# A linear-attention and MoE kernel on one core: bonus term moved to VectorE, state kept block-diagonal, and a scheduler that models the port, the DMA queue and the matmul banks

## The chip, the cores and the metric

The kernel runs on one core of a Trainium2 chip. The metric is the device time of one execution in microseconds. The kernel before takes 244.26 us (median of four runs, 243.75 to 245.22). "PE" is TensorE's matmul stream, "PEld" its weight loads, "DVE" is VectorE, "ACT" ScalarE, "POOL" GpSimd and "SP" SyncE, which issues most of the DMAs. SBUF is the on-chip memory that the engines work from, PSUM the one that PE writes its products to; a "bank" is one of PSUM's parts. A "span" is the length of the profiled execution; times inside it start at 0.

## The reference, cut to what matters

The first half is a recurrent attention with a decay `w` per head and channel and a bonus `u` for the current token; the second half is a two-layer MoE block with a leaky ReLU.

```python
# batch 4, heads 8, sequence 768, head_dim 48
for t in range(S):
    cur = einsum('bhd,bhe->bhde', u * k[t], v[t])
    y[t] = einsum('bhd,bhde->bhe', r[t], state + cur)
    state = w * state + einsum('bhd,bhe->bhde', k[t], v[t])
x = y as 3072 tokens x 384
out = leaky(x @ w_in) @ w_out          # w_in 384 x 2048, w_out 2048 x 384
```

Both kernels cut the sequence into 24 stages of 128 tokens (six for each batch element). A stage scales r and k by powers of w (`q_h`, `k_h`), forms masked products between tokens on PE (`ATm`), adds what comes through the state (`s_bd`) and the bonus (`vs`), and transposes the result into `xT`, from which the MoE matmuls read.

## The kernel before

The program is a list of operations with their dependences, a priority, and a duration guessed by the author. A list scheduler runs over it once, on the host, and fixes the order of instructions on every engine. On the chip each engine works through its list in that order. The guessed durations matter only in that they decide the order.

```python
op("DVE", q_h = raw_r * qdec, 490, base + 2)            # 490 ns is what the scheduler is told
op("DVE", k_h = raw_k * kdec, 490, base + 3)
op("POOL", v_sb <- DMA of v, cast to bf16, 1000, base - 150)
op("POOL", rk  = raw_r * raw_k, 540, base + 4)          # f32, 128 x 384
op("POOL", rku = rk * u_tab,    540, base + 5)
op("DVE", s_b = sum over channels of rku, 490, base + 6)
op("POOL", vs = v_sb * s_b, 540, base + 7)
...                                                     # cut: transposes, ATm
op("DVE", z_st = p_kx + s_st, 290, base + 12)           # state, 48 wide per head
op("DVE", s_st = z_st * wlt, 190, base + 12)
for p in range(2):                                      # into the block-diagonal tile
    op("DVE", tensor_copy(s_bd[64*p:64*p+64, :, D*p:D*p+D], s_st[64*p:64*p+64]), 150, base + 13)
...                                                     # cut: y_sb, xT
bk = ring[0] % NMOE; ring[0] += 1                       # three MoE banks in turn
TILES = [(0, 256), (256, 256)] + [(512 * i, 512) for i in range(1, 6)]
```

## Time and profile before

| | before |
|---|---|
| median time | 244.26 us |
| VectorE busy, last `y_sb` starts | 133.2 us, 159.2 us |
| last `xT` copy starts, from there to the end (MoE alone) | 160.3 us, 82.6 us |
| mean granted PE clock | 0.965 |

From the page of the kernel before: busy time by engine, then five rows of the 40 slices of the span (each digit is a busy share in tenths; `PEclk` is the granted clock in tenths).

```profile
PE 182.6 (75%) x1595; PEld 108.8 (45%) x1608; DVE 133.2 (55%) x230; ACT 111.1 (46%) x194; POOL 100.0 (41%) x115
...
PE   0111543776838886978687779999999999999995
...
DVE  1702887889999999999998999820000000000000
...
POOL 8800296695896786985756834100000000000000
PEclk9999999997985999979997999999999999999999
DMA  6999499986491886977586800012001001101121
```

VectorE stands at 8 or 9 from slice 8 to slice 26 and then stops; PE is full only afterwards. So the kernel has two phases in series: attention at VectorE's pace, then MoE at PE's pace. The same by stretches (kernel before; busy microseconds of each engine in each stretch):

```profile
24.00:90.00 66.00, 42.85 (x492) 30.59 (x493) 59.91 (x95) 25.94 (x53) 48.94 (x52) 0.92 0.84 105
90.00:160.20 70.20, 57.16 (x633) 32.82 (x642) 66.71 (x121) 37.34 (x62) 40.79 (x43) 0.95 0.55 71
160.20:242.90 82.70, 79.62 (x442) 43.19 (x442) 0.00 (x0) 38.46 (x68) 0.00 (x0) 1.00 0.13 48
```

The first column after the stretch is its length; then PE, PE's weight loads, DVE, ACT and POOL. From 24 to 160.2 us VectorE works 126.6 of 136.2 us, PE 100.0. PE was idle for the other 36 us. Up to about 48 us no whole MoE tile was finished; in some 25 of the 36 us, counted from the trace, MoE matmuls of finished tiles were waiting for their turn in PE's fixed list. At 128 us, 17 stages were copied into `xT`; their whole tiles hold 82 us of MoE work (an estimate at the 2.4 columns a ns measured below), and 28 us of it had been done.

VectorE's time is not all work. By tile, kernel before (minimum/median/maximum duration in ns, first and last start in us):

```profile
L387 DVE COPY s_bd<-s_st x40: 189/264/3198, 24.6 to 156.6; 64x192 bf16<-64x192 bf16 x40
L330 DVE TENSOR_TENSOR q_h<-raw_r,qdec x24: 541/559/2684, 7.3 to 151.5; 128x384 bf16<-128x384 f32 x24
L332 DVE TENSOR_TENSOR k_h<-raw_k,kdec x24: 541/617/3082, 9.3 to 154.3; 128x384 bf16<-128x384 f32 x24
L406 DVE TENSOR_TENSOR y_sb<-p_y,vs x24: 542/548/558, 31.1 to 159.2; 128x384 bf16<-128x384 f32 x24
```

The means are 744 ns (`s_bd`), 888 (`q_h`) and 970 (`k_h`). `y_sb`, which reads one operand from PSUM, never takes more than 558. What stretches them is visible in order of time (kernel before; start, duration, engine):

```profile
91.62 0.55 DVE L406 TENSOR_TENSOR y_sb<-p_y,vs 128x384 bf16<-128x384 f32 x1
92.09 2.10 DVE L387 COPY s_bd<-s_st 64x192 bf16<-64x192 bf16 x2
92.09 0.84 POOL L340 TENSOR_TENSOR vs<-v_sb,s_b 128x384 f32<-128x384 bf16 x1
92.88 0.99 POOL L336 TENSOR_TENSOR rku<-rk,u_tab 128x384 f32<-128x384 f32 x1
94.01 1.03 POOL L334 TENSOR_TENSOR rk<-raw_r,raw_k 128x384 f32<-128x384 f32 x1
94.22 1.23 DVE L330 TENSOR_TENSOR q_h<-raw_r,qdec 128x384 bf16<-128x384 f32 x1
```

The two copies take about 0.4 us together when they run alone. Here they take 2.10 us and end 0.3 us after GpSimd's `vs` and `rku`; the next product waits for GpSimd's `rk` in the same way.

### The profile page before, as it was taken

What the parts mean: (1) busy time and instruction counts of PE and PEld (TensorE: products, weight loads), DVE (VectorE), ACT (ScalarE), POOL (GpSimd) and SP (SyncE); (2) the same over time, 40 slices, a digit from 0 to 9 for tenths busy, and PEclk for the clock granted to TensorE, in tenths of its full rate; (3) what the DMA queues carried; (4) which work ended last, traced back from release to release, by engine and by line L of the source; (5) the groups of instructions that cost most, each with busy time, mean ns of one, the idle gap of its engine ahead of it and who ended that gap; (6) DMA issues with size and microseconds to landing.
All of it is one profiled execution on the core that took longest, in us unless ns stands there. A gap on an engine that the chain in (4) does not pass through costs nothing.

```text
span 242.9 us, 3961 instructions
## 1 busy us (share of the span) xinstructions
PE 182.6 (75%) x1595; PEld 108.8 (45%) x1608; DVE 133.2 (55%) x230; ACT 111.1 (46%) x194; POOL 100.0 (41%) x115
## 2 busy tenths in 40 slices
PE   0111543776838886978687779999999999999995
PEld 0111422554626643544344445565455446545562
DVE  1702887889999999999998999820000000000000
ACT  4711120573624534846431658624941971593211
POOL 8800296695896786985756834100000000000000
PEclk9999999997985999979997999999999999999999
DMA  6999499986491886977586800012001001101121
GB/s 131 196 195 205 82 136 173 131 96 70 89 126 34 83 130 99 129 87 85 77 94 136 98 3 0 3 57 72 3 30 68 32 3 65 66 0 35 65 97 66
DMA packets 82034, 20.31 MB, mean 84 GB/s; under 512 B 75872, under 2 KB 81248, under 8 KB 82016
## 3 DMA queue, kind: packets, MB, share of 16 engines
q1 hardware_dynamic: 53520, 14.36, 27.4%
q0 software_dynamic: 27936, 5.51, 26.5%
q10 hardware_dynamic: 560, 0.20, 0.3%
q8 instruction: 12, 0.20, 0.3%
q14 instruction: 6, 0.05, 0.1%
HBM read 20.84 MB, written 4.72 MB: 105 GB/s over the span
## 4 chain that ended last, share of the span: by engine, by line
PE 43%; DVE 36%; DMA 7%; POOL 5%; issue 5%; SPq 3%; ACT 1%; POOLq 0%
PE p_moe L450 22%; PE p_moe L431 15%; DVE s_bd L387 10%; DVE k_h L332 7%; DMA raw_k<-in_k_dram 7%; DVE ATm_0 L363 4%; DVE ATm_1 L363 4%; DVE y_sb L406 3%; DVE s_b L338 2%; DVE q_h L330 2%; SPq L326 2%; POOL rk L334 2%; PE p_t L347 2%; POOL rku L336 2%; DVE s_st L384 1%
## 5 line engine op out<-in xcount | busy, mean ns | idle before, releaser
L431 PE MATMUL p_moe<-xT,w_in_sb 128*128 128x512 bf16 (+1 forms) x323 | 74.1, 369 | 0.5 <-issue 0.2
L450 PE MATMUL p_moe<-w_out_sb,gT 128*128 128x384 bf16 x384 | 68.3, 329 | 0.1
L436 ACT ACTIVATE gT<-p_moe 128x512 bf16<-128x512 f32 (+1 forms) x112 | 58.7, 538 | 19.6 <-PE p_moe L431 15.9
L450 PEld LDWEIGHTS p_moe<-w_out_sb,gT 128*128 128x128 bf16 x384 | 36.8, 99 | 23.1 <-issue 0.5
L431 PEld LDWEIGHTS p_moe<-xT,w_in_sb 128*128 128x128 bf16 x336 | 32.7, 104 | 25.4 <-issue 1.1
L352 ACT ACTIVATE qkT<-p_t 128x1024 bf16<-128x1024 bf16 x24 | 24.5, 1023 | 42.4 <-PE p_t L347 42.4
L340 POOL TENSOR_TENSOR vs<-v_sb,s_b 128x384 f32<-128x384 bf16 x24 | 21.5, 894 | 45.8 <-DVE s_b L338 45.5
L347 PE MATMUL p_t<-ident,q_h 128*128 128x128 bf16 x96 | 10.9, 246 | 29.0 <-DVE k_h L332 28.7
L454 ACT ACTIVATE o_sb<-p_moe 128x384 f32<-128x384 f32 x24 | 11.8, 490 | 43.2 <-PE p_moe L450 43.1
L387 DVE COPY s_bd<-s_st 64x192 bf16<-64x192 bf16 x40 | 29.8, 744 | 0.7
L332 DVE TENSOR_TENSOR k_h<-raw_k,kdec 128x384 bf16<-128x384 f32 x24 | 23.3, 970 | 7.3 <-DMA raw_k<-in_k_dram 7.2
L330 DVE TENSOR_TENSOR q_h<-raw_r,qdec 128x384 bf16<-128x384 f32 x24 | 21.3, 888 | 9.5 <-DMA raw_r<-in_r_dram 6.4
L328 POOL DMA_DIRECT2D v_sb<-in_v_dram x24 | 22.5, 939 | 8.7 <-PE p_y L400 4.1
L334 POOL TENSOR_TENSOR rk<-raw_r,raw_k 128x384 f32<-128x384 f32 x24 | 25.4, 1058 | 1.2 <-DMA raw_k<-in_k_dram 0.5
L336 POOL TENSOR_TENSOR rku<-rk,u_tab 128x384 f32<-128x384 f32 x24 | 24.9, 1036 | 0.1
L414 ACT ACTIVATE xT<-p_kx 128x384 bf16<-128x384 bf16 x24 | 11.8, 490 | 20.5 <-PE p_kx L410 20.3
L347 PEld LDWEIGHTS p_t<-ident,q_h 128*128 128x128 bf16 x96 | 6.3, 107 | 32.7 <-DVE k_h L332 32.0
L363 DVE TENSOR_TENSOR ATm_0<-p_a,mask_f 128x512 bf16<-128x512 f32 x24 | 16.4, 683 | 1.7 <-PE p_a L358 1.4
L410 PE MATMUL p_kx<-ident,y_sb 128*128 128x128 bf16 x72 | 8.9, 239 | 10.8 <-DVE y_sb L406 10.6
L363 DVE TENSOR_TENSOR ATm_1<-p_a,mask_f 128x512 bf16<-128x512 f32 x24 | 16.3, 679 | 0.1
L406 DVE TENSOR_TENSOR y_sb<-p_y,vs 128x384 bf16<-128x384 f32 x24 | 13.2, 548 | 1.7 <-PE p_y L400 1.6
L394 PE MATMUL p_y<-s_bd,qkT 128*128 128x96 bf16 x80 | 7.6, 223 | 8.5 <-DVE s_bd L387 8.3
(42 smaller groups left out, 134.2 us busy)
## 6 DMA issues: line engine op xcount, KB each, us to landing
raw_r<-in_r_dram SPq DMA_DIRECT2D x24, 192.0 KB, 2.8
raw_k<-in_k_dram SPq DMA_DIRECT2D x24, 192.0 KB, 3.4
out_dram<-o_sb SPq DMA_DIRECT2D x24, 192.0 KB, 1.9
v_sb<-in_v_dram POOLq DMA_DIRECT2D x24, 96.0 KB, 4.0
w_in_sb<-in_moe_w_in_dram POOLq DMA_DIRECT2D x6, 256.0 KB, 7.9
w_out_sb<-in_moe_w_out_dram POOLq DMA_DIRECT2D x4, 384.0 KB, 8.7
u_tab<-in_u_dram ACTq DMA_DIRECT2D x1, 192.0 KB, 4.2
lnw<-in_w_dram SPq DMA_DIRECT2D x1, 192.0 KB, 4.0
```

What stands on the lines that cost most here:

```text
L328: op("POOL", lambda: [G.dma_start(vv[:, :, :], src(v))], 1000, base - 150, w=[f"v{vi}"], dma=(f"v{vi}", 16), lat=2600)
L330: op("DVE", lambda: V.tensor_tensor(qh[:, :, 0:D], rr[:, :, :], qdec[:, :, :], ALU.mult), 490, base + 2, w=[f"q{pi}"], r=[f"rr{ri}", "qdec"])
L332: op("DVE", lambda: V.tensor_tensor(kh[:, :, 0:D], rk_[:, :, :], kdec[:, :, :], ALU.mult), 490, base + 3, w=[f"k{pi}"], r=[f"rk{ri}", "kdec"])
L334: op("POOL", lambda: G.tensor_tensor(rk[di][:, :, :], rr[:, :, :], rk_[:, :, :], ALU.mult), 540, base + 4, w=[f"t1{di}"], r=[f"rr{ri}", f" ...
L336: op("POOL", lambda: G.tensor_tensor(rku[di][:, :, :], rk[di][:, :, :], u_tab[:, :, :], ALU.mult), 540, base + 5, w=[f"t2{di}"], r=[f"t1{d ...
L347: last = PE.transpose(p_t[:, 512 * x + 128 * i:512 * x + 128 * i + 128], t[:, 2 * i:2 * i + 2, :].rearrange("p h e -> p (h e)"), ident[:, :])
L352: op("ACT", lambda: ACT.activation(T[:, :, :, :].rearrange("p a i t -> p (a i t)"), p_t[:, :], AF.Copy), 900, base + 9, w=[f"T{di}"], r=[" ...
L363: op("DVE", lambda p=p: V.tensor_tensor(ATm[di][p][:, :, :], p_a[p][:, :].rearrange("p (i t) -> p i t", t=L), mask_f[:, :].unsqueeze(1).to ...
L387: op("DVE", lambda p=p: V.tensor_copy(s_bd[1 - zc][64 * p:64 * p + 64, :, D * p:D * p + D], s_st[1 - zc][64 * p:64 * p + 64, :, :]), 150, ...
L431: op("PE", lambda m=m, fb=fb, bk=bk: PE.matmul(p_moe[bk][:, 0:nt], w_in_sb[:, m, 128 * fb:128 * fb + 128], xT[:, m, t0:t0 + nt], start=(m ...
L436: op("ACT", lambda fb=fb, bk=bk: ACT.activation(gb[:, fb, 0:nt], p_moe[bk][:, 0:nt], AF.Lrelu), nt * 0.8333 + 55, base + fb, w=[f"g{ti % N ...
L450: op("PE", lambda q=q, fb=fb, bk=bk: PE.matmul(p_moe[bk][:, 0:DM], gb[:, fb, 128 * q:128 * q + 128], w_out_sb[:, fb, :], start=(fb == 0), ...
```

## The change

Its intent: take most of GpSimd's SBUF work away, spend fewer VectorE operations on the state, let the next stage's front half run ahead of this stage's back half, hold back ("gate") weight loads that competed with the first inputs, and give the scheduler a truer picture of the machine. The diff, cut to its core:

```diff
-TILES = [(0, 256), (256, 256)] + [(512 * i, 512) for i in range(1, 6)]
+TILES = [(L * i, L) for i in range(NSMALL)] + [(512 * i, 512) for i in range(1, 6)]   # NSMALL = 4, L = 128
 # scheduler
-                    t = max(t, d.end)
+                    t = max(t, d.end + (SLACK if o.eng == "PE" and d.eng != "PE" else 0))   # 250 ns
+            if o.grp is not None and o.grp.first is o:     # a MoE group takes the bank that is free first
+                can = [(g.last.end + SLACK if g else 0.0, b) for b, g in enumerate(held) ...]
+            if o.lock:                                     # VectorE/GpSimd port: one at a time
+                t = max(t, port)
+                port = t + o.dur
+            if o.dma:                                      # one DMA queue with a service time
+                queue = max(queue, t + o.dur + DMA_LEAD) + o.svc
 # stage
-        op("POOL", v_sb <- DMA of v with cast)
+        op("SP",  raw_v <- DMA of v, f32);  op("ACT", v_sb = raw_v, 420)
-        op("POOL", rk = raw_r * raw_k, 540);  op("POOL", rku = rk * u_tab, 540)
+        op("DVE", qk = q_h * k_h, 270, lock=True)          # bf16
+        op("DVE", qku = qk * uw, 270, lock=True)           # uw = w * u, bf16
-        z_st, s_st 48 wide per head; two tensor_copy into s_bd
+        op("DVE", z_st = p_z + s_bd[cur], 490)             # 96 wide per pair of heads
+        op("DVE", s_bd[nxt] = z_st * wlm, 290, lock=True)  # wlm is zero off the diagonal blocks
 ...                                                       # cut: front(n+1) is listed before back(n);
 ...                                                       # weight DMAs and early loads gated; one table preload
```

## The prediction

> **What bounds the kernel now.** Two phases, by the table of stretches. From about 24 to 160 us VectorE is the limit: at 30-150 us it is 93-99% busy, about 5.8 us for each of the 24 attention stages. From 160 us on only PE works, 99% busy, on MoE matmuls. At the start (10-26 us) VectorE waits 7.2 us for raw_k and 6.4 us for raw_r (list of waits) with the DMA row at 9: weights compete with the first inputs.
>
> VectorE's 133 us are inflated. By tile, minimum against mean: s_bd copy 189/744 ns (x40), q_h 541/888, k_h 541/970 (x24): some 42 us exceed the minima. Operations that read PSUM (y_sb 542/548) are not stretched. The Trainium skill, "SBUF — State Buffer", section "SBUF: two separate sides", names an exclusive port lock between VectorE operations with two SBUF inputs (or a two-port mode) and GpSimd; this trace agrees: only such operations stretch, with GpSimd about 80% busy.
>
> **What the change does.**
> - GpSimd loses rk and rku (50 us) and the v DMAs (22 us); vs (24 x 0.84 us) and 12 weight DMAs remain.
> - VectorE loses the s_bd copies (7.6 us uncontended); gains qk and qku, 384-wide bf16 at about 0.35 us (estimate from s_st, 192-wide, 0.245 us): +16 us; z_st and s_st double in width: +5.5 us. Uncontended about 105 us; with vs still locking, about 110. Pipelined starts make about 4.3 us a stage.
> - ScalarE gains 24 casts (about 0.5 us each); it has room.
> - DMA: v becomes f32 loads. One raw load costs about 1.1 us of all engines (queue table), so 3.3 us a stage; with weights (about 19 us, an estimate) the first eight stages need about 46 us: DMA limits the start, less badly than before since loads are gated.
> - Fewer table loads: qdec comes about 1.3 us earlier, and the first q_h/k_h are not stretched (2.1 + 1.8 us before).
> - PE does the same MoE work, about 123 us at full rate. In the changed order, 59 us of it stands before the last attention transpose, against 44 us.
>
> **On the critical path.** The tail: before, the last xT transpose came at 160 us with 78.6 us of MoE behind it; 78.6 x 1.02 + 2.6 us of last copy and store gives the 242.9 us span. After: 63.6 us behind it, 67.3 us with these allowances. So the question is when stage 23 ends. Stage 7's inputs at about 44 us; 16 more stages where VectorE needs 4.3-4.6 us and PE (attention 1.5 + MoE 2.9 us) about 4.5, two nearly equal limits in fixed orders, so about 5.0 us; drain 4 us: 128 us. Span 195, time 197 us.
>
> **Prediction: 197 us, 187 to 209 us; faster by over 2%: 0.97, within 2%: 0.02, slower: 0.01.**
>
> **What would show it.** q_h and k_h near 0.6 us mean; qk and qku near 0.35 us; VectorE busy 105-115 us; GpSimd under 40 us; last y_sb at 120-135 us, PE solid for about 65 us after it; DMA row at 9 until about 45 us; in 50-120 us PE and VectorE both above 80%.
>
> **What would make it wrong.** qk/qku at one element a cycle (0.55 us each, +9 us of VectorE); vs blocking a locked operation every stage (up to +20 us); the start still starved by weights; a granted PE clock under 0.9 in the middle (0.83 at 70-90 us now); PE's fixed order waiting on the ATm or qkT chain. Faster than 187 needs stages under 4.5 us.

## The result, and the profile after

Median 199.28 us (198.38 to 200.80, four runs) against 244.26. The ratio is 0.816, 95% interval 0.810 to 0.822. Here and below a ratio is the mean time of one kernel's fast runs over that of the other's of the same rounds, so it is not quite the ratio of the medians. The kernel before drifted between 244.26 and 246.58 us from job to job, so runs of different jobs are compared by their ratios to it.

From the page of the kernel after, the same rows:

```profile
PE 172.3 (88%) x1624; PEld 107.9 (55%) x1624; DVE 108.2 (55%) x239; ACT 115.1 (59%) x200; POOL 32.9 (17%) x44
...
PE   0323897996599999999999999999999999999994
...
DVE  2547599989989999998998989400000000000000
...
POOL 3414314234111131122131121100000000000000
PEclk9999999999669999999999999999999999999999
DMA  4899999999999799585961111001210121002222
```

By stretches, kernel after (columns as before):

```profile
24.00:70.00 46.00, 40.38 (x561) 29.84 (x559) 43.39 (x93) 33.21 (x59) 12.95 (x16) 0.93 1.05 196
70.00:128.50 58.50, 58.50 (x623) 36.44 (x621) 52.84 (x114) 42.92 (x76) 11.83 (x12) 1.00 0.48 107
128.50:196.30 67.80, 64.88 (x367) 35.51 (x364) 0.00 (x0) 30.08 (x54) 0.00 (x0) 1.00 0.13 47
```

PE is full from 70 us on, while attention still runs. The span fell by 46.6 us in two parts: the last `xT` copy starts at 128.9 us, not 160.3 (31.4 us), and what follows takes 67.4 us, not 82.6 (15.2 us). By tile, kernel after:

```profile
L373 DVE TENSOR_TENSOR q_h<-raw_r,qdec x24: 544/550/1184, 5.7 to 120.8; 128x384 bf16<-128x384 f32 x24
L375 DVE TENSOR_TENSOR k_h<-raw_k,kdec x24: 543/551/1184, 6.2 to 121.2; 128x384 bf16<-128x384 f32 x24
L379 DVE TENSOR_TENSOR qk<-q_h,k_h x24: 343/349/359, 8.8 to 121.8; 128x384 bf16<-128x384 bf16 x24
L450 DVE TENSOR_TENSOR y_sb<-p_y,vs x24: 537/554/559, 15.1 to 127.5; 128x384 bf16<-128x384 f32 x24
```

The stretch is nearly gone (means 603 and 620 ns). At first sight the case is closed: the port was freed, VectorE got faster, and time fell as foretold. The experiments show that this is only half of it.

The starts of `y_sb` show a third part, which no experiment takes alone. In the traces stage 0 starts it at 31.07 us before and 15.14 after, stage 7 at 76.49 and 51.38, stage 23 at 159.20 and 127.47. So of the 31.7 us by which attention ends sooner, 15.9 were won before the first `y_sb`, 9.2 in the next seven stages, and 6.6 in the last sixteen (5.17 and 4.76 us a stage). In the kernel before, VectorE waited at the start for inputs, with the DMA row at 9 and the weight loads under way (kernel before; the bracket is the wait in us and what ended it):

```profile
18.78 0.56 DVE L332 TENSOR_TENSOR k_h<-raw_k,kdec 128x384 bf16<-128x384 f32 x1 [7.18 <-DMA raw_k<-in_k_dram]
23.28 0.56 DVE L330 TENSOR_TENSOR q_h<-raw_r,qdec 128x384 bf16<-128x384 f32 x1 [3.94 <-DMA raw_r<-in_r_dram]
```

The gated loads and the new order of the first stages are the likely cause; what each is worth was not tested.

### The profile page after: what moved, and what is told of

Read it like the earlier page. It is cut to its first block, busy times and chain, and to the rows that moved or that the text cites. A ratio compares the mean times of both kernels' runs of the same rounds, so it can differ in the third digit from the quotient of the medians.

```text
span 196.3 us, 3954 instructions
## 1 busy us (share of the span) xinstructions
PE 172.3 (88%) x1624; PEld 107.9 (55%) x1624; DVE 108.2 (55%) x239; ACT 115.1 (59%) x200; POOL 32.9 (17%) x44
## 4 chain that ended last, share of the span: by engine, by line
PE 79%; DVE 8%; SPq 7%; DMA 3%; ACT 1%; issue 1%
PE p_moe L501 32%; PE p_moe L522 32%; SPq L364 6%; PE p_t L392 5%; DMA raw_k<-in_k_dram 3%; PE p_a L403 3%; PE p_y L444 2%; PE p_y L438 2%; PE p_t L454 2%; DVE k_h L375 1%; PE p_z L416 1%; SPq L334 1%; DVE y_sb L450 1%; DVE s_b L383 1%; DVE ATm_0 L408 1%; DVE ATm_1 L408 1%
## 5 line engine op out<-in xcount | busy, mean ns | idle before, releaser
L522 PE MATMUL p_moe<-w_out_sb,gT 128*128 128x384 bf16 x320 | 54.9, 326 | 0.0
L506 ACT ACTIVATE gT<-p_moe 128x512 bf16<-128x512 f32 x80 | 47.0, 599 | 8.1 <-PE p_moe L501 6.2
L377 ACT ACTIVATE v_sb<-raw_v 128x384 bf16<-128x384 f32 x24 | 12.5, 521 | 12.4 <-DMA raw_v<-in_v_dram 8.7
L373 DVE TENSOR_TENSOR q_h<-raw_r,qdec 128x384 bf16<-128x384 f32 x24 | 14.5, 603 | 6.3 <-ACT qdec L342 3.4
L375 DVE TENSOR_TENSOR k_h<-raw_k,kdec 128x384 bf16<-128x384 f32 x24 | 14.9, 620 | 2.7 <-DMA raw_k<-in_k_dram 2.7
L457 ACT ACTIVATE xT<-p_t 128x384 bf16<-128x384 bf16 x24 | 11.8, 494 | 3.3 <-PE p_t L454 3.2
L383 DVE TENSOR_REDUCE s_b<-qku 128x8 f32<-128x384 bf16 x24 | 13.1, 544 | 0.2
L392 PE MATMUL p_t<-ident,k_h 128*128 128x128 bf16 x96 | 10.2, 234 | 2.8 <-DVE k_h L375 2.7
L522 PE MATMUL p_moe<-w_out_sb,gS 128*128 128x384 bf16 x64 | 12.5, 326 | 0.0
L454 PE MATMUL p_t<-ident,y_sb 128*128 128x128 bf16 x72 | 8.4, 228 | 3.6 <-ACT qkT L397 3.2
L403 PE MATMUL p_a<-qkT 64*128 64x128 bf16 x192 | 10.4, 233 | 1.2 <-ACT qkT L397 1.1
```

What stands on the lines that cost most here:

```text
L373: op("DVE", lambda: V.tensor_tensor(qh[:, :, 0:D], rr[:, :, :], qdec[:, :, :], ALU.mult), 490, base + 2, w=[f"q{pi}"], r=[f"rr{ri}", "qdec ...
L375: op("DVE", lambda: V.tensor_tensor(kh[:, :, 0:D], rk_[:, :, :], kdec[:, :, :], ALU.mult), 490, base + 3, w=[f"k{pi}"], r=[f"rk{ri}", "kde ...
L383: op("DVE", lambda: V.tensor_reduce(s_b[di][:, :], qku[di][:, :, :], AX.X, ALU.add), 470, base + 6, w=[f"s{di}"], r=[f"qku{di}"])
L392: last = PE.transpose(p_t[:, 512 * x + 128 * i:512 * x + 128 * i + 128], t[:, 2 * i:2 * i + 2, :].rearrange("p h e -> p (h e)"), ident[:, :])
L403: last = PE.matmul(p_a[p][:, 128 * i:128 * i + 128], T[64 * p:64 * p + 64, 1, i, :], T[64 * p:64 * p + 64, 0, i, :], start=True, stop=True)
L506: op("ACT", lambda f0=f0, gr=gr: ACT.activation(gb[:, f0:f0 + per, :], p_moe[gr.bank][:, :].rearrange("p (f t) -> p f t", t=nt), AF.Lrelu) ...
```

## The experiments

Two theories. **Lock**: the gain comes from VectorE, whose operations are no longer held up by GpSimd. **Order**: the gain comes from the static order, which in the kernel before was made for durations that the chip does not keep (the scheduler was told 150 ns for a copy that took 744) and so parks MoE matmuls behind attention that runs late. Neither speaks of the earlier start.

Twelve kernels ran, all with correct results. "MoE ahead" is how much MoE work stands in PE's list before the last transpose into `xT`: the columns of those matmuls at 2.4 columns a ns (122.9 us in all; in the tail of the trace after, 48 matmuls of 512 columns took 10.36 us, which is 2.37). VectorE busy, the last `y_sb` and the clock are from each run's profile.

| run | median us | ratio to before (95%) | PE clock | VectorE busy | last `y_sb` | MoE ahead |
|---|---|---|---|---|---|---|
| before | 244.26 | 1 | 0.965 | 133.2 | 159.2 | 44.3 |
| after | 199.28 | 0.816 (0.810-0.822) | 0.983 | 108.2 | 127.5 | 59.3 |
| b_recost | 216.22 | 0.880 (0.872-0.888) | 1.000 | 122.8 | 159.8 | 74.0 |
| b_bonus | 207.62 | 0.844 (0.838-0.849) | 1.000 | 108.9 | 133.7 | 56.5 |
| b_bonus_v | 208.34 | 0.847 (0.842-0.852) | 1.000 | 106.8 | 136.4 | 58.2 |
| a_blind | 206.29 | 0.839 (0.834-0.844) | 0.967 | 104.2 | 129.7 | 52.9 |
| a_bonus_pool | 203.52 | 0.824 (0.817-0.831) | 0.975 | 105.5 | 131.1 | 58.2 |
| a_state_split | 209.44 | 0.851 (0.843-0.858) | 0.949 | 114.3 | 138.6 | 59.5 |
| a_pool_tt | 219.70 | 0.891 (0.885-0.897) | 0.953 | 132.6 | 147.9 | 57.4 |
| a_pool_memset | 201.54 | 0.815 (0.808-0.823) | 0.966 | 109.4 | 129.8 | 57.4 |
| a_ring | 204.73 | 0.835 (0.828-0.841) | 0.974 | 109.9 | 126.5 | 54.8 |
| x_small12 | 192.31 | 0.788 (0.784-0.792) | 1.000 | 106.7 | 126.8 | 64.4 |
| x_split12 | 199.92 | 0.812 (0.805-0.819) | 0.983 | 114.1 | 135.7 | 65.3 |
| x_bonus12 | 193.50 | 0.784 (0.780-0.787) | 0.991 | 105.1 | 128.9 | 65.1 |

In x_split12 and x_bonus12 two runs each, and in a_bonus_pool, a_pool_memset and a_ring one each, were slow; the ratios leave them out, the medians do not. The profile of x_split12 fell in a slow run, so its two trace columns and its clock are only a rough guide. For a_bonus_pool, a_state_split, a_pool_tt and a_pool_memset, what is shown here was read from the recorded profile; the trace kept is of another execution and has VectorE busy for 104.5, 114.6, 131.4 and 109.0 us and the last `y_sb` at 133.4, 138.8, 146.0 and 128.5.

The clock column seems to leave the start out. The profile shows 1.00 there, but the 128x128 transposes of `q_h` and `k_h` took 0.31 us in place of 0.22 up to 47 us in the kernel before, up to 22 in the kernel after, and up to 38 in b_recost, whose clock reads 1.000.

### b_recost: the kernel before, scheduler told the measured durations

```diff
-        op("DVE", q_h ..., 490)      +        op("DVE", q_h ..., 820)
-        op("DVE", k_h ..., 490)      +        op("DVE", k_h ..., 900)
-        op("POOL", rk / rku, 540)    +        op("POOL", rk / rku, 1050 / 1030)
-        op("POOL", vs, 540)          +        op("POOL", vs, 890)
-        op("DVE", copy s_bd, 150)    +        op("DVE", copy s_bd, 670)
```

> The kernel before; only the durations told to the static scheduler are changed, to the means that the trace of before shows (q_h 490 to 820 ns, k_h 490 to 900, s_bd copy 150 to 670, rk and rku 540 to 1050 and 1030, vs 540 to 890). Same instructions in another order: 74 us of MoE matmuls (at full rate) now stand before the last attention transpose, against 44 us. Theory 'lock' (the gain of the change comes from shorter VectorE work): the time stays above 235 us. Theory 'order' (the gain comes from a better static order): last y_sb stays at about 159 us, the tail falls to 49 x 1.02 + 2.6 = 52 us, time about 214 us (210 to 222).

Measured 216.22 us. Not one instruction was added, removed or changed, and 12% of the time went. The lock theory as the whole explanation, which said over 235, fell. By stretches, b_recost (columns as in the table of stretches of the kernel before):

```profile
24.00:90.00 66.00, 51.01 (x573) 34.41 (x577) 58.12 (x102) 35.43 (x72) 51.34 (x54) 1.00 0.89 113
90.00:160.80 70.80, 68.41 (x720) 41.16 (x725) 58.46 (x114) 41.93 (x71) 39.83 (x40) 1.00 0.59 88
160.80:213.50 52.70, 49.39 (x275) 26.92 (x275) 0.00 (x0) 23.45 (x42) 0.00 (x0) 1.00 0.13 46
```

Attention ends where it did (last `y_sb` at 159.8 us), but PE works 119.4 us of the 136.8 before that end (100.0 of 136.2 in the kernel before), and the tail is 52.7 us, not 82.7. The granted clock rose as well, from 0.965 to 1.000, but the two tails both ran at 1.00, so the shorter tail is work that no longer stands in it. VectorE's busy time fell too, from 133 to 123 us: another order brings other collisions.

### b_bonus and b_bonus_v: parts of the change alone

```diff
# b_bonus: the kernel before, and
-        op("POOL", rk ...);  op("POOL", rku ...)
+        op("DVE", qk = q_h * k_h, 270);  op("DVE", qku = qk * uw, 270)
# b_bonus_v: that, and
-        op("POOL", v_sb <- DMA of v with cast)
+        op("SP", raw_v <- DMA of v, f32);  op("ACT", v_sb = raw_v, 420)
```

> The kernel before with one change: the bonus product in bf16 on VectorE (qk, qku) in place of rk and rku on GpSimd. Lock theory: q_h and k_h fall from 0.89/0.97 to under 0.7 us mean, s_bd copies from 0.74 to under 0.35, VectorE busy 133 to about 115 us in spite of 17 us more own work, last y_sb at 130 to 138 us; 56.5 us of MoE precede the last transpose, so the tail is 70 us and the time 202 to 210 us. Order theory: little of the gain, over 225 us.

Measured 207.62 us, as the lock theory said: the copies fell from a mean of 744 to 264 ns, `q_h` and `k_h` to 552 and 580, VectorE to 108.9 us busy although it had 17 us more work of its own, last `y_sb` at 133.7. This edit also brings the durations of those operations close to the guessed ones, so it is not a test of the lock alone, and its order is another: MoE ahead rises from 44.3 to 56.5 us.

> As the run with the bonus on VectorE, and v loaded as f32 on SyncE's queue and cast on ScalarE. 22 us of DMA issue leave GpSimd. If DMA issue on GpSimd also holds the port that VectorE needs, the stretched operations lose their rest and it is 3 us or more faster than the bonus alone; if only GpSimd operations that read SBUF hold it, within 2% of the bonus alone (a heavier f32 load pays back what is won).

Measured 0.847 against 0.844: no difference. Moving v to SyncE and ScalarE wins nothing here. GpSimd's DMA issue does hold up copies, but by little: in b_bonus eight `s_bd` copies took over 300 ns, and seven of them (352 to 582 ns) ended within 0.03 us of the end of a v load's issue. Without those issues the mean copy fell from 264 to 216 ns, 1.9 us over 40 copies. Products of two SBUF tiles (`qk`, `qku`) that overlapped an issue kept their 343 to 359 ns.

### a_blind: the kernel after, scheduler made blind

```diff
-SLACK = 250                                   +SLACK = 0
-            if o.lock: t = max(t, port); port = t + o.dur
-                queue = max(queue, t + o.dur + DMA_LEAD) + o.svc;  o.end = queue + DMA_TAIL
+                o.end = t + o.dur + (2200 if e != "POOL" else 4000)
-        op("POOL", vs, 790)                   +        op("POOL", vs, 540)
```

> The kernel after with its scheduler made blind again: no lock modelled, no DMA queue (flat 2.2 us, 4 us from GpSimd), no slack for PE, vs at 540 ns. Same instructions, other order: 52.9 us of MoE before the last transpose against 59.3. Lock theory: last y_sb within 3 us of 127.5, tail 74 against 67.3, so about 206 us (201 to 210). Order theory: 215 us or more.

Measured 206.29 us, on the number of the lock theory, which here was really a sum of both: last `y_sb` 129.7, 6.4 us less MoE ahead. Knowing the machine better is worth 2.8% of the time (0.839 over 0.816) even where the port hardly collides any more. The loss is at the start: first `y_sb` at 18.34 us in place of 15.14, stage 7's at 58.30 in place of 51.38.

### a_pool_tt and a_pool_memset: is it a lock, and of what?

```diff
+        for _ in range(2):                      # in the kernel after, each stage, behind vs
+            op("POOL", dm_c = dm_a * dm_b, 1000)          # a_pool_tt: 128 x 384 f32
+            op("POOL", memset(dm_c[128 x 1216], 1.0), 1000)   # a_pool_memset instead
```

> The kernel after plus two useless GpSimd products a stage (128 x 384 f32, SBUF to SBUF, about 1 us each, behind vs; nothing reads them). No other engine gets any work. Lock theory: q_h, k_h, qk, qku, s_bd stretch; VectorE busy from 108 to 125 us or more; last y_sb 10 to 25 us later; time 208 to 222 us. Without a lock: 199 to 204 us (57.4 us of MoE before the last transpose against 59.3).

> The control: as the run with two useless GpSimd products a stage, in the same order on every engine, but the GpSimd work is two memsets of about 1 us, which write SBUF and read nothing. If the port lock is taken against VectorE operations with two inputs only by GpSimd operations that read SBUF (so the Trainium skill, SBUF - State Buffer): VectorE records as in after and 199 to 204 us. If any GpSimd operation takes it: as slow as with the products.

The instruction lists of PE and VectorE are the same in both programs. First a_pool_tt, then a_pool_memset: busy time by engine, and two tiles.

```profile
PE 178.2 (82%) x1612; PEld 109.7 (50%) x1624; DVE 132.6 (61%) x239; ACT 116.5 (53%) x200; POOL 83.3 (38%) x94
...
L396 POOL TENSOR_TENSOR dm_c<-dm_a,dm_b x48: 982/1002/1317, 11.5 to 146.5; 128x384 f32<-128x384 f32 x48
L381 DVE TENSOR_TENSOR k_h<-raw_k,kdec x24: 540/1058/2773, 6.4 to 141.4; 128x384 bf16<-128x384 f32 x24
```

```profile
PE 173.3 (86%) x1612; PEld 109.4 (55%) x1624; DVE 109.4 (55%) x239; ACT 115.3 (58%) x200; POOL 84.9 (42%) x94
...
L396 POOL MEMSET dm_c<- x48: 1101/1112/1131, 11.5 to 127.9; 128x1216 f32 x48
L381 DVE TENSOR_TENSOR k_h<-raw_k,kdec x24: 541/550/1619, 6.4 to 123.6; 128x384 bf16<-128x384 f32 x24
```

GpSimd is as busy in one as in the other, and nobody reads what it makes. The products cost VectorE 23 us and the kernel 18 us; the memsets cost nothing that can be told from noise. So the conflict is real, and GpSimd's busy share alone says little. In this pair the operation that *reads* SBUF costs and the one that only writes does not; the two differ in more than that, and no other kind was tried. It agrees with what the Trainium skill, "SBUF — State Buffer", section "SBUF: two separate sides", states for VectorE operations with two SBUF inputs: they contend only with a GpSimd operation that reads SBUF.

### a_bonus_pool and x_bonus12: the bonus term put back

```diff
-        op("DVE", qk ..., 270, lock=True);  op("DVE", qku ..., 270, lock=True)
+        op("POOL", rk ..., 1000, lock=True);  op("POOL", rku ..., 1000, lock=True)
```

> The kernel after with one part undone: the bonus product back on GpSimd in f32 (rk, rku, about 1 us each, told to the scheduler with their lock). VectorE has 17 us less work of its own. Lock theory: q_h, k_h and s_bd stretch again, VectorE busy at or above 108 us although its uncontended work is about 88, last y_sb at 135 to 143 us, 58.2 us of MoE before it, time 206 to 214 us. If only the order counts: 197 to 203 us.

Measured 203.52 us, 0.824 against 0.816, with overlapping intervals: a miss for the lock theory (206 to 214 us). Undone in the finished kernel, the part that alone had won 15.6% costs 1% or nothing. So it was run once more on the best version found (x_small12, below):

> The run with 12 small tiles (0.788 of before) with the bonus product back on GpSimd in f32. Undoing the bonus in the kernel after cost less than was expected (0.824 against 0.816 of before, intervals overlap): with the state in one tile there are no copies left to be blocked, and VectorE gives up 17 us of its own work for about as much stretching. If so it is a wash here too: 0.785 to 0.80 of before, VectorE busy 103 to 108 us, last y_sb at 126 to 131 us (65.1 us of MoE before it, 64.4 with the bonus on VectorE). If the bonus on VectorE was worth more and the low clock of the earlier run hid it: above 0.805.

Measured 0.784 (0.780 to 0.787) with the bonus on GpSimd, 0.788 (0.784 to 0.792) with it on VectorE: a wash. From the page of x_bonus12:

```profile
PE 170.4 (89%) x1908; PEld 120.3 (63%) x1912; DVE 105.1 (55%) x190; ACT 115.5 (60%) x200; POOL 83.9 (44%) x92
```

GpSimd is back at 84 us and `q_h`, `k_h` and `s_bd` are stretched again (means 774, 791 and 522 ns; 14.5 us over their minima), but that costs about what `qk` and `qku` cost (16.8 us): VectorE is busy 105.1 us against 106.7. In the kernel before the stretch was 40.8 us, 22.2 of them in the copies that are gone. The kernel after also tells its scheduler of the lock, and which of the two makes the bonus harmless on GpSimd was not separated.

### a_state_split and x_split12: the two copies put back

```diff
-        z_st, s_bd 96 wide, s_bd[nxt] = z_st * wlm
+        z_st, s_st 48 wide;  two tensor_copy into s_bd[nxt], 150, lock=True
```

> The kernel after with another part undone: state kept 48 wide per head and copied into the block-diagonal tile by two copies a stage. The copies should now take about 0.2 us (no f32 products on GpSimd to collide with), VectorE's busy time within 5 us of 108, 59.5 us of MoE before the last transpose as in after: 197 to 203 us, no clear difference. If the masked multiply were itself worth much, 205 us or more.

A miss: 209.44 us, 0.851 against 0.816. The clock was 0.949, with long stretches at half rate, so the run did not settle it, and x_split12 put the same edit on a kernel whose clock is full after its start:

> The run with 12 small tiles, with the state kept by two copies again. The first run with the split state came out 10 us slower than after, against what was expected, but with the clock at 0.949, not 0.983, and longer lulls. If that clock was the cause: within 2% of the run with 12 small tiles, with a clock above 0.98. If the split state itself costs (28 more PE instructions and two VectorE operations a stage in the chain of a stage): still 3% or more slower at a full clock.

Measured 0.812 against 0.788: still 3.0% slower, from only two fast runs. Their clocks were 0.983 and 0.991, so this clock was not quite full either; but at the same 0.991 one run took 199.40 us here and 192.34 in x_small12. The split state does cost. From a_state_split:

```profile
PE 177.4 (86%) x1692; PEld 111.1 (54%) x1704; DVE 114.3 (55%) x279; ACT 115.2 (56%) x199; POOL 33.8 (16%) x46
...
L432 DVE COPY s_bd<-s_st x40: 190/207/1310, 16.9 to 134.0; 64x192 bf16<-64x192 bf16 x40
```

The copies have a mean of 273 ns, 10.9 us for 40, and the wider sum and product in the kernel after cost only about 4.5 us more than the narrow ones here. VectorE is 6.1 us busier, and it was busy 94 to 96% of the time in the middle of the kernel after. The edit also gives PE eight state matmuls a stage in place of four; how much of the cost is theirs was not tested.

### a_ring: banks in a fixed rotation

```diff
-            gr.first = gr.last = gr.bank = None      # bank chosen when the group is scheduled
+            gr.bank = ring[0] % NMOE; ring[0] += 1   # next in the program's order
```

> The kernel after with the three MoE banks in a fixed rotation in the order of the program, as before, in place of the scheduler's choice. 54.8 us of MoE precede the last transpose, against 59.3: tail about 72 against 67.3 us. If that is all, about 4 to 5 us slower than after (0.83 to 0.845 of before); if PE also waits in front of banks that are not the oldest, 0.85 or more; if the choice is worth nothing, 0.81 to 0.825.

Measured 0.835 against 0.816, 2.3% slower: last `y_sb` at 126.5 as in after (127.5), 4.5 us less MoE ahead, and the profiled span 4.2 us longer. The bank choice is worth what the count of MoE ahead says.

### x_small12: a version faster than both

```diff
-NSMALL = 4;   TILES = [(L * i, L) for i in range(NSMALL)] + [(512 * i, 512) for i in range(1, 6)]
+NSMALL = 12;  TILES = [(L * i, L) for i in range(NSMALL)] + [(512 * i, 512) for i in range(NSMALL // 4, 6)]
```

In the kernel after, PE goes slack at 45 to 55 us: the four 128-token tiles are done, and the next tile needs four whole stages. Kernel after, then x_small12, both in stretches of 5 us (the third column from the right is the granted PE clock):

```profile
45.00:50.00 5.00, 3.19 (x51) 2.02 (x47) 5.00 (x12) 3.16 (x6) 2.40 (x4) 1.00 1.19 209
50.00:55.00 5.00, 3.46 (x36) 2.45 (x37) 4.98 (x13) 1.93 (x3) 1.65 (x2) 0.52 1.13 211
55.00:60.00 5.00, 5.00 (x43) 2.59 (x41) 4.10 (x10) 3.22 (x6) 0.64 (x1) 0.80 0.93 183
```

```profile
45.00:50.00 5.00, 5.00 (x101) 4.65 (x97) 4.80 (x12) 5.00 (x10) 1.77 (x3) 1.00 1.16 187
50.00:55.00 5.00, 5.00 (x100) 4.96 (x96) 4.81 (x13) 4.51 (x9) 1.36 (x2) 1.00 1.14 210
```

> The kernel after with 12 MoE tiles of 128 tokens in place of 4 before the 512-token tiles begin. Every run of the kernel after and its variants shows a lull of PE at about 45 to 55 us, where the four small tiles are done and the first 512-token tile still waits for four stages, and half the clock for 10 to 30 us right behind it. If the lull brings the low clock, the clock is 0.99 or more here (0.983 after). 64.4 us of MoE precede the last transpose (59.3), so the tail is 62 against 67 us: 190 to 195 us, 0.775 to 0.80 of before. If the small tiles' extra weight loads cost as much as they win: 0.81 to 0.83.

Measured 192.31 us, 0.788: 3.5% faster than after. The lull is filled and the clock is 1.000 in three of four runs and 0.991 in the other (0.983, 0.983, 0.974 and 0.983 in those of after). A lower clock behind the lull agrees with the Trainium skill, "TensorE: Matmul & The Clock Gate", "Part 1: The HAM clock gate", where the clock follows PE's recent activity. This run changes the order as well, with 5.1 us more MoE ahead. The traces point to the order: the span is 5.9 us shorter, the last `y_sb` comes only 0.7 us sooner, and both tails ran at 1.00, so some 5.2 us are MoE work that left the tail. A gain of the clock that the extra small tiles ate up again is not ruled out. In the kernel after the half rate lasted some 7 us, shorter than the text above has it (0.54, 0.50 and 0.59 in the stretches of 2.5 us from 50.0 to 57.5).

## Why the prediction was right, and where it was not

The time (197 foretold, 199.28 measured) and nearly all of its marks were right. Its sum was: stage 7's inputs, which wait for DMA; 16 more stages; a drain; a tail read from PE's list.

- Stage 7's `q_h` started at 44.45 us (44 foretold). From the `y_sb` of stage 7 at 51.38 us to that of stage 23 at 127.47 a stage took 4.76 us (5.0 foretold). The last `xT` copy came at 128.9 us (128), and the rest took 67.4 us (67.3). That 128 was met so closely is partly luck: the 16 stages were put 4 us too long, and the drain, from stage 23's `q_h` at 120.8 us to the copy, took 8.1 us, not 4.
- `q_h`, `k_h` at 603 and 620 ns (near 600), `qk` and `qku` at 350 (350), VectorE 108.2 us busy (105 to 115), GpSimd 32.9 (under 40), PE 98% and VectorE 95% busy from 50 to 120 us (both above 80% foretold). The 200 ns between a bf16 product and an f32 one of 384 elements also agrees with the Trainium skill, "VectorE: DVE Perf Modes", "The perf-mode tier table", which has bf16 products at twice the rate of f32 ones.
- It counted the MoE work in PE's list ahead of the last transpose (59 against 44 us). That count, not VectorE's busy time, carried the 15 us of the tail.
- It expected the loads to limit the start less than before, since they are gated. Stage 7's `q_h` started 18.2 us sooner (62.62 to 44.45 us): more than half of what attention won. That the gates did it is not shown.

What was off:

- The step "GpSimd loses rk and rku" as the source of VectorE's gain. The lock is real (a_pool_tt), but in the finished kernel the bonus on GpSimd is as fast (x_bonus12): the 17 us that VectorE takes over are about what the stretching costs once the copies are gone. The move wins a lot only in the kernel before (b_bonus), where it frees the copies as well and brings the durations near to what the scheduler was told.
- The state's term was mis-sized. The text takes 7.6 us off for the copies, at their minimum of 189 ns, and adds 5.5 us for the doubled widths: 2 us won. Measured, the copies cost 10.9 us, and VectorE gains 6.1 us, 3% of the time.
- "DMA row at 9 until about 45 us": it stood there until about 64 us (slice 13 of 40), and after one slice at 7 again until 79. Past 30 us that can have cost VectorE little: it was 94 to 96% busy from then on, up to 110 us.
- The clock. The text feared a middle under 0.9; it came (0.83 from 50 to 70 us) as a few microseconds at half rate at 50 to 58 us, behind a lull that the text had not seen coming.

Not tested alone: the gated loads, the single table preload, the front half of the next stage listed before the back half of this one, the second MoE product two tiles behind the first in place of one, the wide state on the kernel before, and the f32 load of v inside the finished kernel. So the 15.9 us of earlier start have no experiment of their own.

The parts don't add up, and that is the main point. Correct durations alone win 12.0%, the bonus alone 15.6%, the whole change 18.4%. Each of the first two puts more MoE work ahead of the last transpose (74.0 and 56.5 us against 44.3), so they win partly the same time. That a microsecond saved elsewhere is worth less once PE is full from 70 us on is our reading; no run isolates it.

## What to carry to other kernels

When a static schedule runs on the chip, compare the durations that the scheduler was told with those of the trace before changing any instruction: an order made for a fast machine leaves the limiting engine idle on a slow one, and mending the numbers can win most of what a rewrite wins. Split a time into "when does the last dependent stage end" and "how much of the other engine's work is left then"; both can be read before a run. Measure a part of a change by undoing it in the finished kernel as well as by doing it alone, since the two can differ by an order of magnitude.

## What the Trainium skill lacked or had wrong

- "SBUF — State Buffer", "SBUF: two separate sides": the page says that the loser of the shared port waits for the whole instruction of the other. In the kernel before a pair of copies waited 2.10 us behind two GpSimd products that ran one after the other, and a single copy took 3.198 us, from 51.70 us to 0.06 us after the third of three GpSimd products in a row, none of which took more than 1.381 in this trace: the waiting side does not get the port at the next instruction's end for certain.
- The same page: its exception for GpSimd operations that read no SBUF agrees with the one pair of runs here, and they put a number on it: 48 products of 1.0 us cost VectorE 23 us, 48 memsets of 1.1 us cost it about 1 us.
- "TensorE: Matmul & The Clock Gate", "HAM oscillation — how this bites in real kernels": its rule is no idle gap above about 3.4 us. In the kernel after, the clock halved at about 50 us, in a stretch in which PE had records for 64 to 69% of the time (3.19 and 3.46 of 5 us) and no listed wait was above 0.8 us: it fell without such a gap. So this rule alone does not foretell the lull; the page's next section does tell of a clock lost to frequent short idles of PE. What share of busy time keeps the clock full was not measured.
- No page says that the durations given to a static scheduler are worth checking against a trace: correcting six of them won 12% (b_recost, 0.880).
